# A fused attention and two feed-forward kernel: a fixed cyclic order for each engine in the attention, with its own places for the first weight tiles

## The chip, the cores and the metric

The kernel runs on one core of a Trainium2 chip. Its metric is the device time of one execution in microseconds, as the median of several runs. Five engines take part, and each works through its own instructions in the order in which they stand in the program: TensorE (PE, with its weight loads PEld), VectorE (DVE), ScalarE (ACT), GpSimd (POOL), and SyncE (SP), which here only issues DMAs.

## What is computed

Attention with a threshold, then two feed-forward blocks, all in float32:

```
scores = q @ k^T / 8                          # 4 batches x 8 heads, 576 positions, head size 64
thresh = max(scores, row) - tau
attn   = softmax(where(scores >= thresh, scores, -1e9))
x      = (attn @ v) as 2304 tokens x 512
h      = x @ w_in                             # 512 -> 2048
x      = (h * tanh(softplus(h))) @ w_out      # 2048 -> 512
out    = (silu(x @ w_gate) * (x @ w_val)) @ w_out2     # 512 -> 1536 -> 512
```

## The kernel before

**Precision.** A float32 product is made of three matmuls in the narrower type fp32r: an operand is split into a rounded part ("hi") and the rest ("lo"). A weight tile arrives as 64-bit words and is converted to such a pair by ten operations (`Weights.ops`): a load (l), six operations on DVE (a L437, b L440, c L447, d L450, e L454, x L458), one integer addition on POOL between b and d (u, L444), the hi part on ACT (L463) and the lo part, which is on POOL for the first four tiles and on DVE for the others (L468).

**Attention.** The 32 heads are worked in 16 pairs. A pair p has nine score blocks S0 to S8 of 128 queries by 576 keys (`scores`, tile s, L89 on PE, three buffers). For each block i, DVE takes the row maximum (R, L108), POOL makes the threshold (H, L112), ACT the exponential (E, L118), DVE the masked product with its row sum (M, L126, tile pp). PE transposes pp in 14 groups (T, `trans`, tile tg, L149) and ACT copies each group from PSUM (V, `evac`, L155 to L162) into pt. Two products with v follow (A, `av`, L172), one for each half of the queries, with the reciprocal of the row sums (Q on DVE, L182), its spread (rw on POOL, L189), its transposition (B on PE, tile rg, L197) and copy (C on ACT, L205); DVE multiplies the two (x, L210). The tiles tg, rg and av share two PSUM banks (`g`), which they take in turn in a sequence that is written down in `turns`: a tile must wait until the one before the last has been read. The inputs of a pair are loaded by SP (one buffer for q and k together, `n`), scaled (POOL), split in hi (ACT, L219) and lo (POOL, L222), and copied by DMA into a stacked form (`stack`, tile stk, L231, four copies for q and eight for k).

**The order.** `attention` puts all these operations into a `Plan`, which writes the program. An operation has an engine, an assumed cost, what it must wait for, the buffers that it takes and frees, and a rank. `Plan.run` walks through an assumed time: at each step it takes, of the operations that are ready, the one that can start first, or, within a window `WAIT` of 0.2, the one of the lowest rank. The rank is 9 times the number of the pair plus an entry of the table `RANK` for its kind. Beside the attention stand the conversions of the first four weight tiles (`beside`, tiles wraw, cg, cn, early), with one number for a whole tile (`EARLY`), and the split of the first 512 tokens (x0, L722 and L723, with `XEARLY`). The feed-forward part (`moes`) has a plan of its own behind that of the attention.

The core of `Plan.run`:

```
t, e = min((max(clock[e], o["t"]), o["rank"], o["n"], e) for e in engines for o in ready[e])[::3]
t, _, _, o = min(((max(clock[e], o["t"]), o["rank"], o["n"], o) for o in ready[e]
                  if max(clock[e], o["t"]) <= t + self.wait), key=lambda x: x[1:3])
```

Of the kernel before, what the change touches and what calls it, by code (L numbers as in the profile page):

```python
# [20 lines left out]
def f(ap):  # L21
    return ap.bitcast(F32)
# [22 lines left out]
def attention(tc, cst, q, k, v, x, beside=None, S=576):  # L45
# [14 lines left out]
    st = [dict() for _ in range(NP)]  # L60
# [194 lines left out]
    plan = Plan(SLOTS, WAIT)  # L255
    for p in range(NP):
        ranks = {x: iter(y) for x, y in RANK.items()}
        small = iter(range(16))

        def op(eng, cost, fn, *a, key, after=(), take=(), free=()):  # L260
            kind = "first" if p == 0 and key[0] in ("q", "k") else key[0] if eng != "DMA" else "D" + key[0] if key[1] == "load" else "st"
            plan.op(eng, cost, lambda p=p: fn(p, *a), (p, *key), [(p, *x) for x in after], take, free, 9 * p + next(ranks[kind]))

        if p == 0:
            for h in range(2):
# [22 lines left out]
        for i in range(9):  # L288
            c, h = divmod(i, 2)
# [9 lines left out]
            if i in (3, 8):  # L299
                u = int(i == 8)  # L300
# [16 lines left out]
    if beside:  # L317
        beside(plan, place)
    with tc.manual_schedule():
        plan.run()  # L320
    ctx.close()


class Plan:
# [10 lines left out]
        ACT=dict(PE=.216, DVE=.245, ACT=.145, Pool=.16, DMA=.16),  # L335
        Pool=dict(PE=.143, DVE=.06, ACT=.08, Pool=.096, DMA=.08),
# [17 lines left out]
                    n[x[0]] += 1  # L354
                o[to].append(x)

    def run(self):
        made = {o["key"]: o for o in self.ops}
        took = {x: o for o in self.ops for x in o["take"]}
        gave = {x: o for o in self.ops for x in o["free"]}  # L360
        for o in self.ops:
            o["t"], o["then"] = 0.0, []
        for o in self.ops:
            before = [(made[x], True) for x in o["after"] if x not in self.given]
            for x, k in o["take"]:
                if (x, k - 1) in took:
                    before.append((took[x, k - 1], False))
                if k >= self.slots[x]:
                    before.append((gave[x, k - self.slots[x]], True))
            o["left"] = len(before)  # L370
            for y, late in before:
                y["then"].append((o, late))
        engines = {o["eng"] for o in self.ops}
        clock = {e: 1.3 if e == "DMA" else 0.0 for e in engines}
        ready = {e: [o for o in self.ops if o["eng"] == e and not o["left"]] for e in engines}
        n, turn = 0, False
        while any(ready.values()):
            t, e = min((max(clock[e], o["t"]), o["rank"], o["n"], e) for e in engines for o in ready[e])[::3]
            t, _, _, o = min(((max(clock[e], o["t"]), o["rank"], o["n"], o) for o in ready[e] if max(clock[e], o["t"]) <= t + self.wait), key=lambda x: x[1:3])
# [304 lines left out]
@with_exitstack  # L684
def kern(ctx, tc, q, k, v, tau, w_in, w_out, w_gate, w_val, w_out2, out):
    cp = ctx.enter_context(tc.tile_pool(name="c", bufs=1))
    pe = ctx.enter_context(tc.tile_pool(name="w0", bufs=1))
    NT, DM = out.shape
    acc = cp.tile([P, DM // P * NT], F32, name="acc")
    tc.nc.scalar.preload_act_table_set("natural_log_exp_and_others")  # L690
    cst = consts(tc, cp, tau)


    chunks = [(c, min(CHUNK, NT - c)) for c in range(0, NT, CHUNK)]

    def units(groups, one):
        return [dict(one=one, j=j, c0=c0, n=n, g0=g, G=G, lastg=(g, G) == groups[-1]) for g, G in groups for c0, n in chunks for j in range(g, g + G)]

    starts = lambda sizes: [(sum(sizes[:i]), n) for i, n in enumerate(sizes)]
    gr1, gr2 = starts(GROUPS1), starts(GROUPS2)  # L700
    U1, U2 = units(gr1, True), units(gr2, False)

    tiles = []
    for g, G in gr1:
        for i in range(0, G, 2):
            tiles += [(m, j, m is w_out) for m in (w_in, w_out) for j in range(g + i, min(g + i + 2, g + G))]
    for j in range(w_out2.shape[0] // P):
# [24 lines left out]
CHUNK = 512  # L732
# [57 lines left out]
```

## Time and profile before

| | |
|---|---|
| median of 3 runs | 1168.89 us (1168.82 to 1168.99) |
| the profiled execution | 1168.52 us, of which its span is 1166.7 us |
| PE busy | 1122.5 us, 96% of the span |
| DVE busy | 757.0 us, 65% |
| ACT busy | 457.8 us, 39% |
| POOL busy | 246.1 us, 21% |
| attention | from the start to about 314 us |
| feed-forward | from there to the end, about 852 us |

The span counts from the first to the last instruction; 1.8 us lie around it. The shares are means over stages that differ: in the feed-forward part PE is busy nearly throughout, in the first 40 us hardly. "Busy" of PE counts pipelined matmuls whose ends are modelled. The chain that ended last goes back from the last instruction to what released each step.

### The profile page before, as it was taken

Reading aid. Unit: us, or ns where it says so; the run is one execution under the profiler, and the core shown is the slowest. Engines: PE = TensorE matmul, PEld = TensorE weight load, DVE = VectorE, ACT = ScalarE, POOL = GpSimd, SP = SyncE. Lnnn points to the kernel's source line nnn. Section 1 sums busy time; section 2 is a strip of 40 time slices with the busy share of each in tenths; the row PEclk is TensorE's granted clock in tenths of the full one; section 3 lists DMA queues with packets and bytes.
Section 4 is the critical chain, followed back from the end, with each engine's and each line's share of the span. In section 5 each row is a group of like instructions: output and inputs, shape, how many; then the busy total and the mean of one; then the engine's idle time right before and its main releaser. Section 6 shows DMA issues by size and latency. Waiting matters only on the chain.

```text
span 1166.7 us, 16261 instructions
## 1 busy us (share of the span) xinstructions
PE 1122.5 (96%) x6088; PEld 928.0 (80%) x6088; DVE 757.0 (65%) x1375; ACT 457.8 (39%) x897; POOL 246.1 (21%) x368
## 2 busy tenths in 40 slices
PE   1899999999989999999999999999999999999998
PEld 1677787777667888888888888888888888888887
DVE  7988888888689774582752599636426853594333
ACT  3788777787644332232322245333112211222111
POOL 4555444443373110010110031001000200020000
PEclk9999999999989999999999999999999999999999
DMA  6466566565023211110120111202101210120012
GB/s 190 107 154 163 148 164 158 146 169 146 13 67 104 65 37 37 37 54 19 39 71 1 37 55 58 70 1 72 37 1 37 72 55 1 37 72 1 1 72 91
DMA packets 34271, 83.24 MB, mean 71 GB/s; under 512 B 5264, under 2 KB 5264, under 8 KB 34192
## 3 DMA queue, kind: packets, MB, share of 16 engines
q1 hardware_dynamic: 34192, 82.20, 24.9%
q8 instruction: 48, 0.79, 0.3%
q14 instruction: 31, 0.25, 0.1%
HBM read 50.92 MB, written 4.72 MB: 48 GB/s over the span
## 4 chain that ended last, share of the span: by engine, by line
PE 91%; DVE 5%; POOL 2%; issue 1%; ACT 0%; SPq 0%; DMA 0%; ACTq 0%; DVEq 0%
PE h L525 27%; PE y L536 16%; PE v L525 12%; PE y L538 12%; PE s L89 8%; PE tg L149 7%; PE av L172 7%; DVE cg L454 1%; DVE cn L458 1%; PE rg L197 1%; POOL xlo L552 1%; DVE gl L545 1%; DVE cg L450 1%; POOL cg L444 0%; SPq L76 0%
## 5 line engine op out<-in xcount | busy, mean ns | idle before, releaser
L444 POOL TENSOR_TENSOR cg<-cg,ione 128x512 int32<-128x512 int32 x68 | 92.2, 1360 | 627.9 <-DVE cg L440 627.9
L542 ACT CAST gh<-s 128x512 fp32r<-128x512 f32 (+1 forms) x140 | 80.9, 579 | 257.3 <-DVE s L566 126.4
L525 PE MATMUL h<-xhi,wt 128*128 128x512 f32 (+1 forms) x576 | 170.5, 363 | 0.0
L545 DVE TENSOR_TENSOR gl<-s,gh 128x512 fp32r<-128x512 f32 (+1 forms) x140 | 98.9, 708 | 107.6 <-ACT gh L542 106.3
L89 PE MATMUL s<-stk 128*128 128x320 f32 (+5 forms) x672 | 126.2, 317 | 26.1 <-DVE pp L126 14.2
L566 DVE TENSOR_TENSOR s<-v,u 128x512 f32<-128x512 f32 (+1 forms) x60 | 38.0, 634 | 171.5 <-PE v L525 171.5
L89 PEld LDWEIGHTS s<-stk 128*128 128x128 f32 (+1 forms) x672 | 98.3, 190 | 33.6 <-issue 19.9
L108 DVE TENSOR_REDUCE sm<-s 128x1 f32<-128x576 f32 x144 | 108.6, 754 | 24.6 <-PE s L89 24.4
L525 PEld LDWEIGHTS h<-xhi,wt 128*128 128x128 f32 x576 | 104.7, 189 | 17.3
L126 DVE SCALAR_TENSOR_TENSOR pp<-s,sm,e 128x576 f32<-128x576 f32 x144 | 115.9, 806 | 3.6 <-ACT e L118 1.1
L536 PE MATMUL y<-gh,wt 128*128 128x512 f32 (+1 forms) x400 | 113.3, 368 | 0.0
L118 ACT ACTIVATE e<-s,sm 128x576 f32<-128x576 f32 x144 | 109.3, 759 | 8.8 <-DVE sm L108 8.0
L149 PE MATMUL tg<-idf,pp 128*128 128x128 f32 x656 | 104.6, 285 | 3.5 <-DVE pp L126 2.8
L525 PE MATMUL h<-xlo,wt 128*128 128x512 f32 (+1 forms) x288 | 104.5, 363 | 0.0
L155 ACT COPY pt<-tg 128x384 f32<-128x384 f32 x192 | 87.2, 493 | 33.7 <-PE tg L149 33.4
L525 PE MATMUL h<-xhi,early 128*128 128x512 f32 (+1 forms) x320 | 95.0, 363 | 1.1 <-ACT s L557 1.1
L557 ACT ACTIVATE s<-h 128x512 f32<-128x512 f32 (+1 forms) x80 | 44.2, 555 | 124.6 <-PE h L525 121.8
L149 PEld LDWEIGHTS tg<-idf,pp 128*128 128x128 f32 x656 | 73.2, 142 | 23.2 <-ACT qh L219 4.4
L563 ACT ACTIVATE u<-h 128x512 f32<-128x512 f32 (+1 forms) x60 | 33.2, 554 | 147.9 <-PE h L525 147.9
L172 PE MATMUL av<-pt,vn 128*64 128x256 f32 (+1 forms) x640 | 84.7, 411 | 0.0
L536 PEld LDWEIGHTS y<-gh,wt 128*128 128x128 f32 x400 | 72.6, 189 | 12.5
L575 DVE TENSOR_TENSOR acc<-y,acc 128x512 f32<-128x512 f32 (+1 forms) x100 | 60.6, 633 | 29.7 <-PE y L536 29.7
(110 smaller groups left out, 2162.7 us busy)
## 6 DMA issues: line engine op xcount, KB each, us to landing
raw<-in_dram SPq DMA_DIRECT2D x64, 512.0 KB, 3.5
stk<-kh SPq DMA_DIRECT2D x60, 144.0 KB, 2.7
stk<-kl SPq DMA_DIRECT2D x60, 144.0 KB, 2.6
vn<-in_dram SPq DMA_DIRECT2D x16, 320.0 KB, 2.9
out_dram<-acc SPq DMA_DIRECT2D x18, 256.0 KB, 2.0
qn<-in_dram SPq DMA_DIRECT2D x15, 288.0 KB, 3.2
kn<-in_dram SPq DMA_DIRECT2D x15, 288.0 KB, 3.6
stk<-qh SPq DMA_DIRECT2D x30, 144.0 KB, 3.7
```

Of the source, the lines that this page charges most:

```text
L89: nc.tensor.matmul(out=s[out, c0:c0 + n], lhsT=stk[:, 0, qc:qc + out.stop - out.start], rhs=stk[:, w, kc:kc + n], start=w == 1, stop=w == 2)
L108: nc.vector.tensor_reduce(out=d["nm"][:, i:i + 1], in_=d["s", i], op=ALU.max, axis=AX.X, negate=True)
L118: nc.scalar.activation(out=e, in_=d["s", i], func=AF.Exp, bias=d["nm"][:, i:i + 1])
L126: nc.vector.scalar_tensor_tensor(out=d["pp", c][:, 576 * h:576 * h + 576], in0=d["s", i], scalar=d["th"][:, i:i + 1], in1=d["e", i], op0=A ...
L149: nc.tensor.transpose(g[:, 128 * m:128 * m + 128], d["pp", c][:, o:o + 128], idf)
L155: nc.scalar.copy(out=t[:, m0:m0 + n, 128 * (c % 2):128 * (c % 2) + 128], in_=g[:, 0:n])
L172: nc.tensor.matmul(out=d["av", u][64 * h:64 * h + 64, 0:n], lhsT=d["vn"][:, 5 * h + j], rhs=d["pt", u][:, 5 * h + j if j < 4 else 4, 0:n], ...
L444: nc.gpsimd.tensor_tensor(out=g, in0=g, in1=self.ione.to_broadcast([P, 512]), op=ALU.add)
L525: nc.tensor.matmul(out=un[nm], lhsT=w[:, a, P * d:P * d + P], rhs=parts(x, d, un["c0"], un["n"]), start=d == 0 and k == 0, stop=d == ND - ...
L536: nc.tensor.matmul(out=y[:, 0:un["n"]], lhsT=w[:, a, P * d:P * d + P], rhs=x, start=first and k == 0, stop=last and k == 2)
L538: nc.tensor.matmul(out=y, lhsT=x[:, P * d:P * d + P], rhs=w[:, a], start=first and k == 0, stop=last and k == 2)
L545: V.tensor_tensor(out=un["gl"], in0=un["s"], in1=f(un["gh"]), op=ALU.subtract)
```

## The change

The tables are new, and so is the way in which the attention's plan uses them. `run(True)` no longer looks at which operation could start first: every engine has one queue that is sorted by rank alone, and takes its operations in that order, waiting at the head if need be. The rank is now 17.4 times the pair's number plus the entry of the table, so that every pair has the same order on each engine, shifted by one pair. `EARLY` has a number for each of the ten operations of each of the four early weight tiles, and `XEARLY` one for each of the eight splits of the first tokens. No operation is added or taken away, no tile or buffer count changes, and the plan of the feed-forward part is as it was.

```diff
-            plan.op(..., 9 * p + next(ranks[kind]))
+            plan.op(..., PERIOD * p + next(ranks[kind]))
...
-        plan.run()
+        plan.run(True)
...
+        queue = {e: sorted((o for o in self.ops if o["eng"] == e), key=lambda o: (-o["rank"], -o["n"])) for e in engines}
...
+            if strict:
+                heads = [e for e in engines if queue[e] and not queue[e][-1]["left"]]
+                t, _, e = min((max(clock[e], queue[e][-1]["t"]), queue[e][-1]["n"], e) for e in heads)
+                o = queue[e].pop()
...
-EARLY, XEARLY = (-20, -129.8, 314.6, -292.4,), 202.1
+EARLY = ((-483.86, -338.08, -278.01, -546.43, -122.87, -178.15, -136.83, 70.72, 117.99, 177.97), ...)
+XEARLY = (96.93, 265.74, 98.77, 224.23, 304.99, 281.73, 136.71, 302.44)
...
+PERIOD = 17.4
...
-            W.ops(plan, n, {x: EARLY[n] - 20 * (x == "l") for x in ("l", "a", "b", "u", "c", "d", "e", "x", "h", "")}, ...)
+            W.ops(plan, n, dict(zip(("l", "a", "b", "u", "c", "d", "e", "x", "h", ""), EARLY[n])), ...)
```

The order moves at these places. The changed file has eight lines more ahead of `Weights`, so that L437 to L468 of before are L445 to L476 there.

**DVE, the first score blocks of pair 0.** In s0_1 the first number is the pair, the second the block; cg1 and cn1 are tiles of the early weight tile 1. L108 is R, L126 is M. Before:

```order
L437 TENSOR_SCALAR cg0_111<-wraw0_110 128x512
L437 TENSOR_SCALAR cg1_120<-wraw1_119 128x512
L440 SCALAR_TENSOR_TENSOR cg1_120<-wraw1_119,cg1_120 128x512
L108 TENSOR_REDUCE sm0_157<-s0_0_138 128x1
L108 TENSOR_REDUCE sm0_157<-s0_1_146 128x1
L447 TENSOR_SCALAR cn1_121<-wraw1_119 128x512
L126 SCALAR_TENSOR_TENSOR pp0_0_168,sm0_157<-s0_0_138,sm0_157,e0_0_161 128x576
L450 TENSOR_SCALAR cg1_120<-cg1_120 128x512
L454 SCALAR_TENSOR_TENSOR cg1_120<-wraw1_119,cg1_120 128x512
L458 SCALAR_TENSOR_TENSOR cn1_121<-cn1_121,cg1_120 128x512
L440 SCALAR_TENSOR_TENSOR cg0_111<-wraw0_110,cg0_111 128x512
L447 TENSOR_SCALAR cn0_112<-wraw0_110 128x512
```

Now:

```order
L445 TENSOR_SCALAR cg1_122<-wraw1_121 128x512
L246 TENSOR_TENSOR stk0_108<-kd0_98,stk0_108 64x576
L455 TENSOR_SCALAR cn1_123<-wraw1_121 128x512
L108 TENSOR_REDUCE sm0_156<-s0_0_142 128x1
L108 TENSOR_REDUCE sm0_156<-s0_1_151 128x1
L126 SCALAR_TENSOR_TENSOR pp0_0_175,sm0_156<-s0_0_142,sm0_156,e0_0_167 128x576
L108 TENSOR_REDUCE sm0_156<-s0_2_158 128x1
L126 SCALAR_TENSOR_TENSOR pp0_0_175,sm0_156<-s0_1_151,sm0_156,e0_1_173 128x576
L108 TENSOR_REDUCE sm0_156<-s0_3_182 128x1
L126 SCALAR_TENSOR_TENSOR pp0_1_203,sm0_156<-s0_2_158,sm0_156,e0_2_191 128x576
L108 TENSOR_REDUCE sm0_156<-s0_4_196 128x1
L126 SCALAR_TENSOR_TENSOR pp0_1_203,sm0_156<-s0_3_182,sm0_156,e0_3_210 128x576
```

Before takes 21 of the 24 conversion operations of DVE between the first maximum of pair 0 and the fifth (its last ones stand behind these rows); now none stands there. Of tile 0 the operations a, b, d, e and c, and of tile 1 a and c, stand ahead of the first maximum; x of tile 0 comes behind the seventh M, and 14 of the others among pairs 1 to 13, one or two at a place, with four between the sixth and the ninth R of pair 5. The last two (e and x of tile 3) stand behind R and x of pair 15's last block and first half.

**PE, the second half of a pair's turn**, here the first blocks of pair 9 beside the second product of pair 8. Before:

```order
L89 MATMUL s9_5_2469<-stk9_2113 128x320 x2
L89 MATMUL s9_5_2469<-stk9_2113 128x256 x2
L149 MATMUL tg9_0_0_2487<-idf_63,pp9_0_2400 128x128 x3
L149 MATMUL tg9_0_3_2491<-idf_63,pp9_0_2400 128x128 x3
L89 MATMUL s9_6_2498<-stk9_2113 128x320 x2
L89 MATMUL s9_6_2498<-stk9_2113 128x256 x2
L149 MATMUL tg9_0_6_2506<-idf_63,pp9_0_2400 128x128 x3
L149 MATMUL tg9_1_0_2513<-idf_63,pp9_1_2459 128x128 x3
L89 MATMUL s9_7_2521<-stk9_2113 128x320 x2
L89 MATMUL s9_7_2521<-stk9_2113 128x256 x2
L149 MATMUL tg9_1_3_2528<-idf_63,pp9_1_2459 128x128 x3
L172 MATMUL av8_1_2535<-pt8_1_2337,vn8_2316 64x320 x10
```

Now:

```order
L149 MATMUL tg9_0_0_2451<-idf_63,pp9_0_2381 128x128 x3
L89 MATMUL s9_5_2458<-stk9_2082 128x320 x2
L89 MATMUL s9_5_2458<-stk9_2082 128x256 x2
L149 MATMUL tg9_0_3_2470<-idf_63,pp9_0_2381 128x128 x3
L149 MATMUL tg9_0_6_2476<-idf_63,pp9_0_2381 128x128 x3
L89 MATMUL s9_6_2481<-stk9_2082 128x320 x2
L89 MATMUL s9_6_2481<-stk9_2082 128x256 x2
L149 MATMUL tg9_1_0_2489<-idf_63,pp9_1_2437 128x128 x3
L149 MATMUL tg9_1_3_2494<-idf_63,pp9_1_2437 128x128 x3
L89 MATMUL s9_7_2500<-stk9_2082 128x320 x2
L89 MATMUL s9_7_2500<-stk9_2082 128x256 x2
L172 MATMUL av8_1_2510<-pt8_1_2317,vn8_2295 64x320 x10
```

The first transposition of pair 9 moves ahead of S5, and those that stood as 0_0 with 0_3 and 0_6 with 1_0 now stand as 0_3 with 0_6 and 1_0 with 1_3, so that none is left between S7 and the product av8_1. In the other half of the turn, from av8_1 to S4 of the next pair, PE's order is the same in both.

**ACT, beside it.** e9_2 is the exponential of block 2, pt the copy of a transposition group (V), rs the copy C. Before:

```order
L118 ACTIVATE e9_2_2446<-s9_2_2412,sm9_2359 128x576
L158 COPY pt8_1_2337<-tg8_4_0_2441 128x4x64 x2
L118 ACTIVATE e9_3_2462<-s9_3_2430,sm9_2359 128x576
L205 COPY rs8_1_2474<-rg8_1_2464 128x320
L162 COPY pt8_1_2337<-tg8_4_4_2449 64x64 x2
L118 ACTIVATE e9_4_2484<-s9_4_2452,sm9_2359 128x576
L155 COPY pt9_0_2486<-tg9_0_0_2487 128x3x128
L155 COPY pt9_0_2486<-tg9_0_3_2491 128x3x128
L118 ACTIVATE e9_5_2511<-s9_5_2469,sm9_2359 128x576
L155 COPY pt9_0_2486<-tg9_0_6_2506 128x3x128
L155 COPY pt9_0_2486<-tg9_1_0_2513 128x3x128
```

Now:

```order
L118 ACTIVATE e9_2_2422<-s9_2_2390,sm9_2345 128x576
L158 COPY pt8_1_2317<-tg8_4_0_2417 128x4x64 x2
L162 COPY pt8_1_2317<-tg8_4_4_2426 64x64 x2
L118 ACTIVATE e9_3_2442<-s9_3_2409,sm9_2345 128x576
L205 COPY rs8_1_2456<-rg8_1_2444 128x320
L155 COPY pt9_0_2450<-tg9_0_0_2451 128x3x128
L118 ACTIVATE e9_4_2474<-s9_4_2430,sm9_2345 128x576
L155 COPY pt9_0_2450<-tg9_0_3_2470 128x3x128
L155 COPY pt9_0_2450<-tg9_0_6_2476 128x3x128
L155 COPY pt9_0_2450<-tg9_1_0_2489 128x3x128
L118 ACTIVATE e9_5_2522<-s9_5_2458,sm9_2345 128x576
```

The two copies of tg8_4_4 move ahead of E3 and of C, and the exponential E5 moves behind the copy of tg9_1_0.

On POOL the lo part of k of the next pair moves behind the threshold H2, and on SP the load of the next but one pair's q moves ahead of the eight copies of k into the stack; on SP at the start, the load of the first weight tile moves ahead of q and of half of k.

## Rows read from the trace of the kernel before

**Rows 1.** Page section 4: who holds the chain that ended last, over the span

```profile
PE 91%; DVE 5%; POOL 2%; issue 1%; ACT 0%; SPq 0%; DMA 0%; ACTq 0%; DVEq 0%
```

**Rows 2.** Windows, one pair: us, then busy of PE, PEld, DVE, ACT, POOL

```profile
160.13:177.41 17.28, 17.15 (x132) 13.47 (x134) 14.22 (x33) 13.66 (x30) 7.50 (x17) 1.00 0.61 153
```

**Rows 3.** Windows, DVE alone, at the start of the attention

```profile
5.50:13.90 8.40, 7.41 (x13) 1.00 0.92 323
13.90:46.34 32.44, 30.86 (x51) 1.00 0.41 108
```

**Rows 4.** Lines, DVE, 5.5 to 13.8 us: busy us, mean ns | idle before

```profile
L437 DVE TENSOR_SCALAR cg<-wraw 128x512 int32<-128x512 int32 x2 | 0.7, 411 | 0.0
```

**Rows 5.** Lines, DVE, 13.9 to 46.34 us, the conversions alone

```profile
L458 DVE SCALAR_TENSOR_TENSOR cn<-cn,cg 128x512 f32<-128x512 f32 x4 | 6.8, 1705 | 0.1
L454 DVE SCALAR_TENSOR_TENSOR cg<-wraw,cg 128x512 int32<-128x512 int32 x4 | 3.5, 871 | 0.1
L440 DVE SCALAR_TENSOR_TENSOR cg<-wraw,cg 128x512 int32<-128x512 int32 x3 | 2.1, 687 | 0.1
L437 DVE TENSOR_SCALAR cg<-wraw 128x512 int32<-128x512 int32 x2 | 2.1, 1036 | 0.0
L450 DVE TENSOR_SCALAR cg<-cg 128x512 int32<-128x512 int32 x4 | 1.7, 432 | 0.0
L447 DVE TENSOR_SCALAR cn<-wraw 128x512 int32<-128x512 int32 x4 | 1.7, 416 | 0.0
```

**Rows 6.** Timeline: start us, us; first maxima, pair 1's last stack copy, first av

```profile
13.80 1.55 DVE L108 TENSOR_REDUCE sm<-s 128x1 f32<-128x576 f32 x2
...
28.98 0.59 SPq L231 DMA_DIRECT2D stk<-kh  x1
...
46.34 2.38 PE L172 MATMUL av<-pt,vn 128*64 128x256 f32 x20
```

**Rows 7.** Chain that ended last, within one pair: start us, us, what

```profile
164.66 0.22 PE rg L197 x2
...
165.75 0.66 PE tg L149 x6
...
172.79 0.13 issue
172.92 0.41 PE rg L197 x2
...
174.09 0.80 PE tg L149 x6
...
175.48 0.93 PE tg L149 x6
176.41 0.53 PE s L89 x4
...
177.41 2.84 PE av L172 x19
```

**Rows 8.** Timeline of ACT in the same pair

```profile
173.86 0.42 ACT L162 COPY pt<-tg 64x64 f32<-64x64 f32 x2
...
175.68 0.77 ACT L118 ACTIVATE e<-s,sm 128x576 f32<-128x576 f32 x1
176.31 0.88 ACT L155 COPY pt<-tg 128x384 f32<-128x384 f32 x2
```

**Rows 9.** Timeline, later: a conversion while POOL waits, and POOL (brackets: idle before)

```profile
348.70 0.68 DVE L458 SCALAR_TENSOR_TENSOR cn<-cn,cg 128x512 f32<-128x512 f32 x1
...
351.12 1.42 POOL L444 TENSOR_TENSOR cg<-cg,ione 128x512 int32<-128x512 int32 x1 [2.89 <-DVE cg L440]
```

**Rows 10.** Timeline at the end of the attention: brackets give idle before

```profile
313.96 0.49 DVE L210 TENSOR_TENSOR acc<-av,rs 128x320 f32<-128x320 f32 x1 [5.55 <-PE av L172]
...
315.23 7.66 POOL L552 TENSOR_TENSOR xlo<-acc,xhi 128x512 fp32r<-128x512 f32 x5 [8.21 <-ACT xhi L549]
```

**Rows 11.** DMA issues, 160 to 178 us: KB each, us to landing

```profile
stk<-kh SPq DMA_DIRECT2D x4, 144.0 KB, 2.7
```

More of the change, by code (lines that the diff above doesn't have):

```diff
@@ L261, in op @@
             kind = "first" if p == 0 and key[0] in ("q", "k") else key[0] if eng != "DMA" else "D" + key[0] if key[1] == "load" else "st"
-            plan.op(eng, cost, lambda p=p: fn(p, *a), (p, *key), [(p, *x) for x in after], take, free, 9 * p + next(ranks[kind]))
+            plan.op(eng, cost, lambda p=p: fn(p, *a), (p, *key), [(p, *x) for x in after], take, free, PERIOD * p + next(ranks[kind]))
         if p == 0:
@@ L355, in op, with run @@
                 o[to].append(x)
-    def run(self):
+    def run(self, strict=False):
         made = {o["key"]: o for o in self.ops}
@@ L377, in run @@
         while any(ready.values()):
-            t, e = min((max(clock[e], o["t"]), o["rank"], o["n"], e) for e in engines for o in ready[e])[::3]
-            t, _, _, o = min(((max(clock[e], o["t"]), o["rank"], o["n"], o) for o in ready[e] if max(clock[e], o["t"]) <= t + self.wait), key=lambda x: x[1:3])
+            if strict:
+                heads = [e for e in engines if queue[e] and not queue[e][-1]["left"]]
+                t, _, e = min((max(clock[e], queue[e][-1]["t"]), queue[e][-1]["n"], e) for e in heads)
+                o = queue[e].pop()
+            else:
+                t, e = min((max(clock[e], o["t"]), o["rank"], o["n"], e) for e in engines for o in ready[e])[::3]
+                t, _, _, o = min(((max(clock[e], o["t"]), o["rank"], o["n"], o) for o in ready[e] if max(clock[e], o["t"]) <= t + self.wait), key=lambda x: x[1:3])
             ready[e].remove(o)
@@ L404 @@
 TURN = 0.16
-EARLY, XEARLY = (-20, -129.8, 314.6, -292.4,), 202.1
+EARLY = ((-483.86, -338.08, -278.01, -546.43, -122.87, -178.15, -136.83, 70.72, 117.99, 177.97), (83.95, -59.96, 90.15, 99.11, 59.63, 161.34, 195.41, 211.82, 268.18, 353.64), (90.77, 120.32, 234.39, 218.66, 154.26, 250.85, 252.39, 292.87, 286.81, 297.74), (110.51, 128.14, 159.04, 177.67, 155.41, 208.84, 339.2, 348.67, 441.07, 594.86),)
+XEARLY = (96.93, 265.74, 98.77, 224.23, 304.99, 281.73, 136.71, 302.44)
 SLOTS = dict(wraw=3, wc=6, sm=4, wt=4, s=3, g=2, e=4, pp=3, pt=2, rw=6, rs=6, vn=1, stk=2, n=1, hl=2)
-RANK = dict(P=(-1107.5, -3856.5,), S=(1554.8, 4238.1, -1560.9, 6102.6, 2908.6, 4102, 775.3, 522.3, 4206.5,), R=(-497.8, -3340.3, 669.6, 3608.3, 3026, 717.8, 831.5, 928.3, 4030.3,), H=(-886, -444.4, 1030.3, -4229.5, -2589.8, 349.5, 1807.7, 1355.9, 213.1,), E=(3368.6, 3927.2, 1695.2, -673.1, 1498.6, 1776.5, -593.4, 669.3, -846.5,), M=(-1175.9, 2946.4, 945.8, -609.9, -2796.2, -3324.4, 4863.3, -385.9, -1034.2,), T=(-478.2, 4203, 1183.7, -3198.6, 4629, -1326.8, 1256.1, -915.3, -1499, 4366.2, -87.2, 1989.7, -1057.9, -309.2,), V=(42.7, -4071.5, -346.7, 5127, 3454.4, 6389, -3685.4, 995.6, 2605, 958.3, 1465.4, 344.9, -629.1, 846.5,), Q=(3107.2, -1624.9,), rw=(1354.7, 2037.2,), B=(1328.8, -3213.1,), C=(2643.5, -837.5,), x=(-1547.1, -1257.1,), A=(-860.3, 2598.4, 29.5, 62, 62, 62,), Dq=(520.6,), Dk=(-2288.5,), Dv=(290.4,), q=(932.4, 1295.4, 1207.3,), k=(5062.6, -143.8,), st=(1990.4, -587.4, -280.8, 262.9,), first=(-1663.3, -753.4, -565, -1886.6, -1082, -513.8, -1127.5, -1209, -547.5, -548.2, -763.4, -797.9, 477.9, -1762.2, -1379.4, -1091.3, -1322.9, -672.5,))
@@ new lines @@
+PERIOD = 17.4
+RANK = dict(first=(-150.78, -113.2, -142.86, -586.82, -261.67, -483.31, -79.57, -91.85, -103.43, -30.22, -70.26, -241.87, -475, -167.25, -572.12, -358.96, -89.37, 39.96,), Dv=(104.87,), S=(51.58, 53.03, 55.88, 57.93, 60.26, 61.92, 64.49, 66.32, 67.51,), R=(60.32, 62.49, 63.91, 64.41, 64.83, 66.99, 67.49, 67.88, 74.38,), H=(31.01, 31.63, 33.94, 37.26, 37.57, 42.48, 43.86, 46.73, 47.34,), E=(49.67, 50.13, 52.21, 54.15, 58.31, 61.56, 62.03, 62.51, 66.92,), M=(63.39, 64.14, 64.74, 65.4, 65.77, 69.33, 70.2, 72.29, 79.94,), T=(60.89, 62.99, 63.66, 65.52, 65.67, 67.32, 68.41, 69.58, 69.95, 71.81, 73.46, 74.38, 75.41, 75.54,), V=(57.48, 58.36, 58.69, 60.09, 61.84, 64.65, 65.74, 66.17, 66.77, 68.68, 69, 69.09, 70.12, 71.33,), P=(42.9, 49.1,), Q=(70.19, 81.22,), rw=(43.95, 50.72,), B=(67.86, 78.15,), C=(65.44, 73.17,), A=(73.23, 84.04,), x=(81.26, 87.85,), Dq=(62.1,), q=(6.71, 28.1, 12.36,), Dk=(73.05,), k=(34.04, 17.47,), st=(73.06, 74.1, 80.63, 84.66,))
@@ L718, in beside @@
         for n in range(NEARLY):
-            W.ops(plan, n, {x: EARLY[n] - 20 * (x == "l") for x in ("l", "a", "b", "u", "c", "d", "e", "x", "h", "")}, place, ["wraw"], ["wraw"], ["wc"], ["wc"], "Pool")
+            W.ops(plan, n, dict(zip(("l", "a", "b", "u", "c", "d", "e", "x", "h", ""), EARLY[n])), place, ["wraw"], ["wraw"], ["wc"], ["wc"], "Pool")
         for d in range(DM // P):
             a, h, l = x[:, d, 0:CHUNK], x0[0][:, d], x0[1][:, d]
-            plan.op("ACT", .093 + CHUNK / 1200, lambda a=a, h=h: tc.nc.scalar.copy(out=h, in_=a), ("x0", d), [(d, "x", 0), (d, "x", 1)], [], [], XEARLY)
-            plan.op("Pool", .04 + CHUNK / 418, lambda a=a, h=h, l=l: tc.nc.gpsimd.tensor_tensor(out=l, in0=a, in1=f(h), op=ALU.subtract), ("X0", d), [("x0", d)], [], [], XEARLY)
+            plan.op("ACT", .093 + CHUNK / 1200, lambda a=a, h=h: tc.nc.scalar.copy(out=h, in_=a), ("x0", d), [(d, "x", 0), (d, "x", 1)], [], [], XEARLY[2 * d])
+            plan.op("Pool", .04 + CHUNK / 418, lambda a=a, h=h, l=l: tc.nc.gpsimd.tensor_tensor(out=l, in0=a, in1=f(h), op=ALU.subtract), ("X0", d), [("x0", d)], [], [], XEARLY[2 * d + 1])
     attention(tc, cst, q, k, v, x, beside)
```

## The prediction

> **What bounds the kernel now.** I read the page's chain first: PE holds 91% of it [rows 1], so only a stretch in which PE waits can give anything, and the feed-forward part, which this change leaves as it is, gives nothing. What is left is the attention, some 314 us, and it has two faces. From the first product with v at 46.34 [rows 6] it is a cycle of one turn per pair, 17.28 us each, in which PE is busy 17.15 and DVE 14.22 [rows 2]. Ahead of that, PE hardly works. The windows of DVE show why: between 13.9 and 46.34 us DVE is busy 30.86 of 32.44 us [rows 3], and the lines show that 21 conversions of weight tiles make 6.8 + 3.5 + 2.1 + 2.1 + 1.7 + 1.7 = 17.9 us of it [rows 5]. They stand in DVE's queue among the maxima of the first pair, and every maximum, mask, transposition and product of the attention waits behind them. These weights are wanted only at 314 us.
>
> **Term 1, the start.** DVE's queue is the path from the first maximum at 13.80 to the first av at 46.34 [rows 6]. Of the 21 conversions there, one stays (x of the first tile, one L458). Its two prices are 0.68 us, where POOL waits [rows 9], and 1.7 us, the mean at the start [rows 5]; I take 1.2, between them. So 17.9 - 1.2 = 16.7 us leave the path. Ahead of the first maximum stood two L437 and one L440; now seven operations stand there, four more: d, e and two c, by the means of rows 5 about 0.43 + 0.87 + 0.42 + 0.42 = 2.1 us. DVE was idle 8.40 - 7.41 = 1.0 us in that stretch [rows 3], which they can fill, so 1.1 us are added: 15.6 us of gain, 15.5 for short. The load of the first weight tile now goes ahead of q and half of k and may cost some tenths more. Two bounds. The best is that the kept L458 is short and the four are hidden: 17.9 - 0.7 = 17.2. The worst: pair 1 can't start before its stacks are there. In before the last of these copies is issued at 28.98 and takes 0.59 [rows 6], and such a copy lands 2.7 us after its issue [rows 11]: 32.3; with the score and transposition that stand between, the first av could come at about 33.3, a gain of 13. That chain gets no longer by the change, since it begins with the load and split of pair 1's q and k, on POOL and ACT, from which conversions are taken as well. If the tiles' DVE time is gone, it is this chain that is late next. Ends: -13 and -17.2; taken: **-15.5 us**.
>
> **Term 2, the turn.** In a turn PE loses time at four places that the chain shows: 0.13 of idle time and 0.41 instead of 0.22 for two transpositions of the reciprocals (rg), then 0.80 and 0.93 instead of 0.66 for six transpositions (tg) [rows 7]: 0.73 us. All four lie in the second half, from rg at 172.92 to av at 177.41, 4.49 us. They are waits for one of the two PSUM banks, which ACT empties: each tg waits for the copy of the tile before the last. The rest of the turn keeps its order on PE and shows no such loss. So I follow ACT from 172.92 in the new order, with the steps that the old one shows: E 0.63 (from 175.68 to 176.31), a copy V 0.44 (half of 0.88), the two small ones 0.42 [rows 8]. The order now is small copies, E3, C, V, E4, V, V, V: in before E5 too stood ahead of the copy that av's bank waits for, and now it stands behind. With C as long as a V: 0.42 + 0.63 + 0.44 + 0.44 + 0.63 + 0.44 + 0.44 = 3.44 us to the copy of tg_0_6, so tg_1_3 can start at 176.36; it takes half of 0.66, S7 0.53 [rows 7], and av starts at 177.22 instead of 177.41: 0.19 us. There are 15 such turns: **-3 us**. Ends: none at all, if another of these waits grows by as much; and the whole 0.73, 15 x 0.7 = 10.5 us, if no bank is late.
>
> **Term 3, the conversions in their new places.** 14 of them now lie among pairs 1 to 13: three each of b and d, two each of a, c, e, x. Short (0.69, 0.43, 0.41, 0.42, 0.69, 0.68 [rows 4, 5, 9]) they make 7.8 us, at the means of the start 11.4 us [rows 5]. DVE has 17.28 - 14.22 = 3.06 us idle in a turn [rows 2], and the most that meet are four (b, d and two c, about 2.0 us). The cover is DVE's idle time at the points where it waits for PE; where one stands at a point where PE waits for DVE, it costs its length. Ends: 0 and half of the long sum, 5.7; taken **+0.5**, near the lower end, because the idle time of 13 turns (40 us) is over three times the long sum.
>
> **Term 4, the end of the attention.** The last e and x of tile 3 stand on DVE where it idled 5.55 us for av; the last hi and lo parts fall into the 8.21 us in which POOL waited for ACT [rows 10]. Nothing is added; the feed-forward part then starts as before, from the same state. 0.
>
> Moved on POOL and SP: the lo part of k behind one threshold, a load of 0.3 to 0.6 us ahead of eight stack copies. Both delay the stacks of the next pair, which are wanted only half a turn later; 0.
>
> **The sum:** -15.5 - 3 + 0.5 = -18.0 us. The profiled execution took 1168.52, 0.4 below the median of the runs; 1168.5 - 18.0 = **1150.5 us**. All ends together: 1140.8 and 1161.2.
>
> **The rule that speaks against it.** An L458 takes 1.7 us at the start and 0.68 where POOL waits [rows 5, 9], and POOL is busy 7.50 of each 17.28 us [rows 2]; so the 14 conversions may well meet POOL's work, and be long. The Trainium skill, GPSIMD Engine Reference, section Specifications, says the same as a rule: POOL shares its SBUF interfaces with DVE and contends with DVE instructions that have two SBUF inputs or use both ports. The rows agree with it. By that rule the long sum holds, and rival B is what it makes.
>
> **Rivals.**
> A: the turn does not get shorter, since the waits for the banks only change their place. For it: ACT is busy 13.66 of 17.28 [rows 2], and E3 now stands ahead of C. Only the start gains: 1168.5 - 15.5 + 0.5 = 1153.5.
> B: the conversions in the turns meet POOL and lie on the path whole: 1168.5 - 15.5 - 3 + 11.4 = 1161.4. Against it: the idle time above.
> C, slower: DVE becomes the bound. M4 now stands directly behind M3 and must wait for E4, which on ACT stands behind E3, C and a copy; three maxima follow it in a row, for which PE must be ahead. The price is DVE's idle time at these heads. It takes over where waits pass 3.06 us in a turn, and outweighs the start where they pass it by more than 15.5/15 = 1.0, so at 4.1 us. One E, C and one V make 0.77 + 0.44 + 0.44 = 1.65 [rows 8], under half of that. With 5 us a turn is 19.2 us: 15 x 1.94 = 29 - 15.5, 1182.
> D: the start is held by its loads. The first tile's half megabyte goes ahead of q and k, the first maximum waits for that and the 2.1 us, and the stacks of pair 1 for this: 13 less 2.1, a gain of 11, and no more: 1168.5 - 11 - 3 + 0.5 = 1155.
> That the change does nothing can be left out: the printed order shows the conversions gone from the start.
>
> **How the numbers follow.** The forecast has 0.60, A 0.18, B 0.08, D 0.10, C 0.04. Faster than 0.2% (2.3 us, about what can be told from no change) are all but C: with a little for what none of them names, faster 0.95, same 0.01, slower 0.04. The range goes from 1143, three quarters of the way to the best end, to 1159, which takes in A, D and most of the way to B; C and the rest of B are left out.
>
> **What will show it.** Right: no L458 group of four among the first maxima; the first av at 30 to 32 us; av to av 17.0 to 17.2 us; 852 us from the last av on, as before. Term 1 is wrong if av starts after 34, and then the row to look at is what S1 of pair 1 waits for. Term 2 is wrong if the turn is 17.28 or if the tg groups of six still take 0.8 to 0.9. Term 3 is wrong if turns with conversions are longer than turns without. A turn above 18.3 us would be rival C.

## The result, and the profile after

The changed kernel takes 1150.08 us, the median of five runs (1148.86 to 1151.23), against 1168.89 before (five runs, 1168.80 to 1168.99): a ratio of 0.984 (95% interval 0.9825 to 0.9854). The profiled execution took 1150.61 with a span of 1148.8, so its span is 17.9 us shorter. The forecast was 18.0 less; the total came out almost to the tenth. Its terms did not, as the rows show. Of the runs below, one execution of no_conv, the traced one, took 3945.72 us, with TensorE's matmuls more than twice as long throughout, and is left out.

The chain that ended last, by engine (for [rows 1]):

```profile
PE 90%; DVE 5%; POOL 2%; issue 1%; ACT 1%; DMA 1%; SPq 0%; DVEq 0%; POOLq 0%; ACTq 0%
```

PE holds as much of it as before. What changed lies where PE waited. The timeline of DVE at the start, for [rows 3, 6] (start, us, instruction, idle time before it):

```profile
11.44 1.82 DVE L246 TENSOR_TENSOR stk<-kd,stk 64x576 fp32r<-64x576 f32 x1
...
15.33 1.95 DVE L246 TENSOR_TENSOR stk<-kd,stk 64x576 fp32r<-64x576 f32 x1
...
17.54 0.74 DVE L108 TENSOR_REDUCE sm<-s 128x1 f32<-128x576 f32 x1
...
29.69 0.69 DVE L466 SCALAR_TENSOR_TENSOR cn<-cn,cg 128x512 f32<-128x512 f32 x1
```

The first maximum now comes at 17.54 instead of 13.80, but from there to the first av (33.04) it is 15.5 us instead of 32.54. The one L466 that stayed is short. DVE no longer holds this stretch; another chain now does. In order of time, up to the first av:

```profile
21.02 1.37 POOL kl L222
...
22.42 4.54 DMA qn<-in_dram
...
27.13 0.74 POOL qn L216
27.87 0.25 POOL sm L112
...
29.03 1.48 PE s L89 x10
...
33.11 1.44 PE av L172 x11
```

The lo part of pair 1's k (kl) frees the one buffer in which q and k are split; only then is the load of pair 2's q issued (4.54 us). On POOL its scaling (qn) stands ahead of a threshold (sm) of pair 0, DVE's mask waits for that threshold, and PE for the mask.

One turn in the windows view (as [rows 2]), and its second half in the chain (as [rows 7]):

```profile
59.68:76.52 16.84, 16.72 (x132) 13.39 (x134) 14.29 (x32) 14.62 (x32) 7.32 (x18) 1.00 0.58 159
```

```profile
156.87 0.41 PE rg L197 x2
...
157.45 0.34 PE tg L149 x3
157.79 0.53 PE s L89 x4
158.32 0.82 PE tg L149 x6
159.13 0.53 PE s L89 x4
159.66 0.86 PE tg L149 x6
160.53 0.53 PE s L89 x4
161.06 2.03 PE av L172 x13
```

The turn is 16.84 us. Between rg and av there are 4.19 us instead of 4.49: the groups of six tg still take 0.82 and 0.86, but the group of three that took 0.48 ahead of av now stands behind rg and takes 0.34, and the two s that took 0.59 and 0.58 take 0.53. Another 0.14 is saved in the first half (12.65 instead of 12.79 from av to rg), and that is one group: the three tg ahead of the pair's first product, before and now:

```profile
166.93 0.46 PE tg L149 x3
```

```profile
151.01 0.33 PE tg L149 x3
```

At the end of the attention DVE idles for av as before ([rows 10]: 5.55 us), and the feed-forward part starts 3.58 us after the last av (3.57 before):

```profile
294.14 0.49 DVE L210 TENSOR_TENSOR acc<-av,rs 128x320 f32<-128x320 f32 x1 [4.95 <-PE av L172]
```

### The profile page after: what moved, and what is told of

Same layout as the page of the kernel before. It is cut to its first block, busy times and chain, and to the rows that moved or that the text cites. A ratio compares the mean times of both kernels' runs of the same rounds, so it can differ in the third digit from the quotient of the medians.

```text
span 1148.8 us, 16265 instructions
## 1 busy us (share of the span) xinstructions
PE 1115.2 (97%) x6088; PEld 925.8 (81%) x6088; DVE 753.7 (66%) x1375; ACT 456.3 (40%) x897; POOL 246.7 (21%) x368
## 4 chain that ended last, share of the span: by engine, by line
PE 90%; DVE 5%; POOL 2%; issue 1%; ACT 1%; DMA 1%; SPq 0%; DVEq 0%; POOLq 0%; ACTq 0%
PE h L533 28%; PE y L544 16%; PE v L533 13%; PE y L546 12%; PE s L89 7%; PE av L172 6%; PE tg L149 6%; PE rg L197 1%; DVE cg L462 1%; POOL xlo L560 1%; DVE gl L553 1%; POOL cg L452 1%; DVE cg L458 0%; DVE cn L466 0%; DMA qn<-in_dram 0%
## 5 line engine op out<-in xcount | busy, mean ns | idle before, releaser
L126 DVE SCALAR_TENSOR_TENSOR pp<-s,sm,e 128x576 f32<-128x576 f32 x144 | 115.6, 810 | 11.6 <-ACT e L118 9.6
L533 PEld LDWEIGHTS h<-xhi,wt 128*128 128x128 f32 x576 | 104.7, 189 | 17.4
L108 DVE TENSOR_REDUCE sm<-s 128x1 f32<-128x576 f32 x144 | 105.7, 754 | 16.2 <-PE s L89 16.0
L118 ACT ACTIVATE e<-s,sm 128x576 f32<-128x576 f32 x144 | 103.2, 753 | 7.8 <-DVE sm L108 7.2
L149 PE MATMUL tg<-idf,pp 128*128 128x128 f32 x656 | 102.0, 280 | 0.3
L571 ACT ACTIVATE u<-h 128x512 f32<-128x512 f32 (+1 forms) x60 | 33.3, 555 | 148.5 <-PE h L533 148.5
L544 PEld LDWEIGHTS y<-gh,wt 128*128 128x128 f32 x400 | 72.5, 189 | 12.6
```

The costliest lines, as they stand in the source:

```text
L108: nc.vector.tensor_reduce(out=d["nm"][:, i:i + 1], in_=d["s", i], op=ALU.max, axis=AX.X, negate=True)
L118: nc.scalar.activation(out=e, in_=d["s", i], func=AF.Exp, bias=d["nm"][:, i:i + 1])
L126: nc.vector.scalar_tensor_tensor(out=d["pp", c][:, 576 * h:576 * h + 576], in0=d["s", i], scalar=d["th"][:, i:i + 1], in1=d["e", i], op0=A ...
L149: nc.tensor.transpose(g[:, 128 * m:128 * m + 128], d["pp", c][:, o:o + 128], idf)
L533: nc.tensor.matmul(out=un[nm], lhsT=w[:, a, P * d:P * d + P], rhs=parts(x, d, un["c0"], un["n"]), start=d == 0 and k == 0, stop=d == ND - ...
L544: nc.tensor.matmul(out=y[:, 0:un["n"]], lhsT=w[:, a, P * d:P * d + P], rhs=x, start=first and k == 0, stop=last and k == 2)
```

## The experiments

The table gives the start of the first av, the 14 turns between the starts of the second product (av, u = 1) of pair 0 and that of pair 14, and the median of the runs.

| run | first av | turns | us | ratio to before |
|---|---|---|---|---|
| before | 46.34 | 17.27 to 17.29 | 1168.9 | |
| changed | 33.04 | 16.84, one 17.18 | 1150.1 | 0.984 |
| turn_back | 34.97 | 18.9 to 21.4 | 1187.9 | 1.016 |
| turn_pe | 35.30 | 17.5 to 17.9 | 1161.0 | 0.993 |
| turn_act | 35.70 | 19.4 to 22.2 | 1208.9 | 1.034 |
| turn_dve | 35.16 | 18.1 to 19.6 | 1171.6 | 1.002 |
| turn_old | 36.28 | 17.30 to 18.28 | 1163.8 | 0.995 |
| old_early | 47.64 | 17.29 to 17.81 | 1173.4 | 1.003 |
| conv_early | 46.68 | 16.83 to 16.84 | 1163.1 | 0.995 |
| no_conv | | | 1149.9 | 0.984 |
| tile0_late | 32.45 | 16.84, two longer | 1148.5 | 0.982 |
| start_n2 | 29.80 | 16.84 to 17.07 | 1145.5 | 0.980 |
| after_again | 34.03 | 16.84, one 16.93 | 1149.9 | 0.983 |

**Undoing one engine's order.** First the places that term 2 spoke of, on PE (T) and ACT (E, V) together, in turn_back, and on each alone, in turn_pe and turn_act:

```diff
-T=(60.89, 62.99, 63.66, 65.52, 65.67,    E: 58.31, 61.56, 62.03,    V: 70.12, 71.33,)
+T=(62.0, 62.99, 65.0, 65.52, 66.5,        E: 58.31, 58.5, 62.03,     V: 70.12, 73.5,)
```

> The changed kernel with the second half of a turn back in its old order on two engines: on PE S5 ahead of the first tg, S6 ahead of the third, S7 behind tg_1_0; on ACT E5 ahead of E-independent copies and the small copies behind C. Theory 1 (the turn is shorter because of these orders on PE and ACT): av to av goes back from 16.84 to about 17.28 us, the first av stays at 33.0, total 1150.1 + 15 x 0.44 = 1156.7 (1155 to 1158). Rival (the turn is shorter because of something else, the order of DVE or POOL, or the conversions' places): av to av stays at 16.8 to 16.9, total 1150 to 1151.

> Only PE's second half is back in its old order, ACT keeps the new one. Theory 1a (ACT's order makes the turn short, as in the prediction): av to av at most 16.95, total up to 1152. Rival 1b (PE's order does it: S5 between the first two tg gives a bank its time): av to av 17.2 or more, total 1155 to 1158.

> Only ACT's second half is back in its old order, PE keeps the new one. Theory 1a (ACT's order does it): av to av 17.2 or more, total 1155 to 1158. Rival 1b (PE's order does it): av to av at most 16.95, total up to 1152.

All three came out above every expected total: the old pieces on PE cost 0.73 us a turn in the mean, those on ACT 3.6, both together 2.5, where the whole old cycle was only 0.44 slower than the new one. Not all of the 3.6 is the order. TensorE's granted clock fell to its lower level again and again in turn_act; the turns in which it stayed at 1.00 take 19.4 us, 2.6 more than in the new cycle, and the others are the longer ones. Two turns of turn_act, next to each other (granted clock third from the end):

```profile
68.95:88.38 19.43, 16.91 (x132) 13.47 (x131) 14.32 (x31) 14.82 (x33) 7.46 (x17) 1.00 0.55 138
88.38:109.93 21.55, 19.03 (x133) 14.50 (x132) 14.87 (x33) 14.67 (x32) 8.52 (x18) 0.90 0.50 133
```

In turn_back, too, the turns of 20.0 us and more are those with a lower clock; the others take 18.9 to 19.3. The chain of turn_pe shows how a piece of the old order costs time (one turn):

```profile
147.44 0.34 PE tg L149 x3
...
148.18 0.75 ACT e L118
148.93 0.38 ACT pt L155
...
149.35 0.55 PE tg L149 x3
```

PE wants the bank of the next tg; on ACT an E stands ahead of the copy that empties it. In turn_act the same wait passes through a third engine:

```profile
166.22 0.76 ACT e L118
...
167.07 0.82 DVE pp L126 x2
167.90 0.68 DVE sm L108
...
168.66 0.74 ACT e L118
169.40 0.38 ACT pt L155
```

E4, then on DVE M4 and the maximum behind it, then E5, then the copy that PE's tg waits for: DVE's new order has M4 ahead of R5, and so E5 must not stand early. So the price of one engine's order depends on the others'.

PE's whole order is the old one in turn_pe, but ACT's is not in turn_back and turn_act: E4 still stands behind the copy of tg_0_0 there, as in the new order. ACT's two orders differ at further places than the printed ones, too, and these stay new: E6 behind the copy of tg_1_3, E8 behind those of tg_2_3 and tg_2_6, and E1 ahead of that of tg_3_0. What ACT's whole old order costs alone was not measured.

Then DVE's order alone (turn_dve; its main difference is below, others lie among R1, M8, M0 and M1), and the cycle of before on DVE, ACT, POOL and PE as a set (turn_old):

```diff
-DVE: R4 M3 M4 R5 R6 R7 M5
+DVE: R4 M3 R5 M4 R6 M5 R7
```

> The changed kernel with only DVE's cyclic order taken back (M4 behind R5, M5 behind R6). Theory 1'' (a turn is as short as the worst fit between the orders; DVE's old order then asks for M5 ahead of R7, while ACT gives E5 late): av to av 17.5 us or more, total above 1158. Rival (DVE has 2.5 us to spare in a turn, so its order does not matter): av to av 16.84 to 16.95, total 1150 to 1152.

> The changed kernel, start and conversions as there, but the cyclic order of one pair on DVE, ACT, POOL and PE all taken from the kernel before, word for word (SP keeps the new one). Theory 1' (the four orders belong together, and the old set as a whole costs 17.28 us a turn): first av at 33 to 35, av to av 17.2 to 17.35, total 1156 to 1159. Rival (it was no order but the old planner's choices from pair to pair, or SP's order): av to av at 16.9 or less, total 1150 to 1152.

turn_dve came out on its theory's side: 18.24 us a turn in the mean, although DVE has 2.5 us to spare in a turn. turn_old has the turns that its theory asks for in four cases, 17.30 to 17.33, and no mixture has a turn under 17.5; but ten turns are 17.37 to 18.28, so that the mean (17.61) is no better than turn_pe's 17.57 and the total is 1163.8. The expectation was only half right. Last, the same order with the conversions taken out of the turns:

```diff
-EARLY: b 90.15, 234.39, 159.04   d 161.34, 250.85, 208.84   x 70.72, 211.82, 292.87, 348.67   ...
+EARLY: b 63.82, 63.83, 64.14      d 63.82, 63.83, 64.42      x 63.82, 63.83, 63.83, 64.44      ...
```

> The kernel with the old cycle on DVE, ACT, POOL and PE (as in the run of that name), and in it the 14 conversions back among the first maxima (as in the run with the conversions early). With that run, the changed kernel and the one with the old cycle it makes four cases: old or new cycle, conversions early or late. Theory I (the old cycle without conversions in it is 17.28 us; the conversions made 8 of the 14 turns longer there, since its order leaves no place where they cost nothing): every turn 17.25 to 17.35, the first av at 47 to 49, total 1169 to 1171. Rival (the old cycle is uneven in this kernel by itself, with a first pair in fixed order): turns of up to 17.8 here too, total 1173 or more.

Eight turns are 17.29 to 17.30 now, the others up to 17.81, and 1173.4 is what the rival said. (The edit takes 16 operations back and not 14: e and x of tile 3 as well, which the changed kernel has at the end of the attention.) So the conversions are not the only thing that makes the old cycle uneven. The chain of its third turn names one other:

```profile
97.51 0.21 ACT pt L155
...
97.89 0.62 ACT early L471
...
99.05 0.49 ACT pt L155
...
99.58 0.55 PE tg L149 x3
```

A hi part of a weight tile (L471), which has its place from the new cycle, stands on ACT among the copies that PE waits for. In conv_early the same casts lie in the new cycle, and there every turn is 16.83 to 16.84. This is one turn; what lengthens the others is not shown.

**The start.** In conv_early only the conversions go back, again 16 of them with e and x of tile 3, and the cycle stays new:

> The changed kernel with the 14 conversions on DVE (and the POOL steps between them) back among the first maxima, the loads of tiles 2 and 3 moved up with them; the hi and lo parts stay late. Theory 2 (DVE's queue is the path to the first av): the first av goes from 33.0 to 41 to 45 us, by 7.8 us at the short durations and 11.4 at the long ones, total 1158 to 1162, the turn stays 16.84. Rival (pair 1's loads and stacks hold the first av): the first av at 36 or earlier, total at most 1153.

The first av came at 46.68, 13.6 later, and the total 13.0 higher: the path through DVE is shown, but its price was above my range. The lines of DVE from 17.5 to 46.68 show most of it (count, busy us, mean ns, idle before):

```profile
L466 DVE SCALAR_TENSOR_TENSOR cn<-cn,cg 128x512 f32<-128x512 f32 x4 | 2.8, 690 | 0.1
L455 DVE TENSOR_SCALAR cn<-wraw 128x512 int32<-128x512 int32 x3 | 2.5, 818 | 0.0
L462 DVE SCALAR_TENSOR_TENSOR cg<-wraw,cg 128x512 int32<-128x512 int32 x3 | 2.1, 693 | 0.1
...
L458 DVE TENSOR_SCALAR cg<-cg 128x512 int32<-128x512 int32 x3 | 1.3, 422 | 2.1 <-POOL cg L452 2.1
```

The operations are nearly all short; with L448 (2.1) and L445 (0.8) they make 11.6 us. One L466 (0.7) of these stands there in the changed kernel too, and one L455 (0.4) stood ahead of the first maximum; so the 16 make 10.5, of which e and x of tile 3 are 1.4, and 2.1 more go in waiting for POOL's step between b and d. That is 12.6 of the 13.6; the last 1.0 is open. Set beside turn_old and old_early, taking the conversions out of the start is worth 13.0 us in the new cycle and 9.6 in the old one.

**The conversions in the turns.**

```diff
+            if k in (1, 2, 3) and s and s in "budex":
+                continue
```

> The changed kernel without the steps b, d, e, x and the POOL step of tiles 1 to 3: 12 operations of DVE and 3 of POOL are left out of the turns (the three tiles then hold other numbers). Theory 3 (DVE's idle time hides them, as the prediction's +0.5): total 1149.6 to 1150.1, turns of 16.84 throughout. Rival B (they lie on the path whole): total 1140 to 1145.

1149.9 us (1149.87 to 1150.66) against 1150.1 and 1149.9 of the kernel with them: no difference that can be told. Ten of the 12 operations stand in the turns of the changed kernel, the other two (e and x of tile 3) at the end; the length of the turns without them is not known. Rival B falls.

**What holds the first av now.** The first two lines are tile0_late; start_n2 has the rest too, with the loads of tiles 0 to 2 at 105 to 110 and the conversions of tiles 0 and 1 a turn or so later than in tile0_late (FIX replaces a rank).

```diff
-EARLY = ((-483.86, -338.08, -278.01, -546.43, -122.87, -178.15, -136.83, 70.72, ...
+EARLY = ((80.5, 68.12, 107.55, 116.51, 84.66, 178.74, 212.81, 229.22, ...
...
-SLOTS = dict(... rw=6, rs=6, vn=1, stk=2, n=1, hl=2)
+SLOTS = dict(... rw=6, rs=5, vn=1, stk=2, n=2, hl=2)
+FIX = {(1, 'k', 'load'): 79.6, (1, 'k', 'hi'): 45.6, (1, 'k', 'lo'): 30.5}
```

> The changed kernel with the load of tile 0 behind that of pair 1's q and its conversions, with a and c of tile 1, moved into the turns too (tile 3 follows later, since it takes tile 0's buffer). Theory 4 (what stands ahead of the first maximum is on the path): the first maximum comes at 13 to 14 us instead of 17.5, the first av at 29 to 30 instead of 33.0, total 1146 to 1147. Rival D (pair 1's loads and stacks hold the first av): the first maximum comes as early, the first av not before 32, total 1149 or more.

> The changed kernel with all weight tiles' loads behind pair 1's stacks, no conversion ahead of pair 1's maxima, two buffers instead of one for the q and k being split (one buffer fewer for the copied reciprocals, for room), and pair 1's k load, cast and lo part directly behind those of q. Theory D (with the conversions gone from the start, pair 1's chain of load, split and stack holds the first av): the first maximum at 13.5 to 14, the first av at 29 to 30 instead of 32.5 in the run with tile 0 late, total 1145 to 1147. Rival (the first pair's own waits between ACT, PE and DVE hold it): the first av at 32 or later, total 1148 to 1150.

In tile0_late the first maximum came at 13.72, 3.8 earlier, and the first av only 0.6 earlier. Its chain has the link seen above:

```profile
20.00 4.76 DMA qn<-in_dram
...
24.93 0.75 POOL qn L216
25.68 0.26 POOL sm L112
...
26.84 1.48 PE s L89 x10
...
30.21 1.28 PE tg L149 x6
```

But it lets PE start on this s at 26.84, and in the changed kernel that was at 29.03: 2.2 us earlier. What follows up to the first av is the same work, and it took 5.6 us against 4.0. The six tg took 1.28 where the changed kernel has 0.66, because TensorE's granted clock was at its lower level in this execution (third number from the end):

```profile
28.00:30.00 2.00, 2.00 (x12) 2.00 (x11) 1.14 (x3) 0.85 (x2) 1.25 (x2) 0.58 0.37 139
30.00:32.00 2.00, 2.00 (x11) 2.00 (x11) 0.76 (x1) 0.96 (x3) 0.27 (x1) 0.56 0.85 266
```

So of the 3.8 us, some 1.6 were lost to the clock and 1.6 to the chain, and the first av of 32.45 can't decide between theory 4 and rival D. The link in the chain is another than rival D named: the load of pair 2's q, not pair 1's stacks. In start_n2, with a second buffer, pair 1's k moved up and the tiles' loads and conversions later, that load is off the chain, PE starts on this s at 25.79, and the first av comes at 29.80, as expected. Which of the three moves takes it off was not tested singly. The chain of start_n2 at the same place:

```profile
23.75 0.23 ACT e L118
...
24.39 0.49 ACT pt L155
...
24.91 0.66 DVE pp L126
...
25.79 1.48 PE s L89 x10
```

It is work of pair 0 itself. start_n2 is the fastest of all: 1145.52 us, 0.980 of before (0.9784 to 0.9813), and 4.4 us under after_again, which ran beside it and has its first av 4.2 later.

**The feed-forward part.** It should have been left as it is, but from its first product to the end it took 854.1 us (294.69 to 1148.8) instead of 852.2 (314.50 to 1166.7).

> The changed kernel as it is, profiled once more. Theory C (the 1.6 us lost after the first accumulation in the feed-forward part are TensorE at the 1.2 GHz level for some 4 us at 338 to 342, which does not happen in every execution): from the first feed-forward product to the end 852.3 us if the granted clock stays 1.00 there, 854.1 if it falls; single times spread over 1.5 to 2.5 us. Rival (the new order itself costs it, each time): 854 in this execution too, with the clock at 1.00.

The same kernel took 852.6 there this time. Windows of the changed kernel, then of its second execution (the last three numbers: granted clock, DMA share, GB/s):

```profile
338.00:340.00 2.00, 1.87 (x5) 1.49 (x6) 1.97 (x5) 2.00 (x6) 0.00 (x0) 0.56 0.37 70
340.00:342.00 2.00, 2.00 (x7) 1.57 (x6) 2.00 (x3) 1.08 (x3) 1.42 (x1) 0.58 0.48 193
```

```profile
338.00:340.00 2.00, 1.07 (x5) 0.90 (x6) 2.00 (x5) 2.00 (x5) 0.00 (x0) 1.00 0.26 107
```

In the first, PE waited 2.02 us for ACT to free its accumulator and then ran some 4 us at a granted clock of 0.56 to 0.58, near its lower level of 1.2 GHz: nine matmuls of y took 3.92 us, against 2.34 in before, where the wait was 1.59 and the clock stayed at 1.00. In the second it stayed at 1.00 too, behind a wait of 1.46. The length of the wait is not what decides: in conv_early PE waited 2.02 us at this place as well, and the clock stayed at 1.00:

```profile
351.00:353.00 2.00, 1.67 (x7) 1.41 (x8) 1.97 (x5) 2.00 (x5) 0.00 (x0) 1.00 0.29 43
```

The feed-forward part, whose order is the same in all these runs, took 852.3 to 852.6 us in each of their other traced executions. So the 1.6 us are a matter of the execution, not of the order; the remaining 0.3 to 0.4 were not followed.

## Why the prediction was right, and where it was wrong

By its own terms, in the profiled execution (in brackets the second one, 1148.1):

| term | forecast | measured |
|---|---|---|
| 1, to the first av | -15.5 (-13 to -17.2) | -13.3 [-12.3] |
| 2, the turn | -3 (0 to -10.5) | -6.9 |
| 3, conversions in the turns | +0.5 (0 to 5.7) | +0.4 [+0.25] |
| 4, the end of the attention | 0 | 0.0 |
| feed-forward | 0 | +1.9 [+0.4] |
| sum | -18.0 | -17.9 [-18.6] |

That the total agrees so closely is luck: errors of about 2, 4 and 2 us cancel. That the start and the turn would both gain was right; their sizes were not, nor was the place in the turn. The first av was to come at 30 to 32 us and the turn to be 17.0 to 17.2; they were 33.04 and 16.84.

**Term 1** was mis-sized. Its main part, the DVE time that leaves the path from the first maximum on, was forecast at 16.7, and the stretch became 17.0 shorter, though DVE was no longer what held it. The step that failed is the 1.1 us added ahead of the first maximum: it was 3.7, and 5.0 in the second execution. The last four of DVE's five lo parts of the first q and k (L246) took 5.6 us together, against 4.1 in before; the two of 1.82 and 1.95 ran beside two-input steps of POOL (10.97 to 12.64, 15.25 to 16.67), another, at 13.18, took 0.75. And the load of tile 0 ahead of q stood ahead of those: the second k landed at 10.06 (8.41 in tile0_late, without it), and 1.2 later in the second execution, where the first av too is 1.0 later. tile0_late shows how much of this counts: with the first maximum 3.8 earlier, PE comes to the last stretch before the first av 2.2 earlier; the chain of the next pairs' loads takes back the rest. The worse bound, that pair 1's stacks let no av start before about 33.3, has nearly the measured number (33.04), but by luck: the link that holds is the load of pair 2's q. Rival D, that the loads hold the start and leave it a gain of 11, had the kind of cause right and the link and the size wrong.

**Term 2** was mis-sized by more than half, and by its own sign (groups of six tg that still take 0.8 to 0.9) its mechanism was wrong too. The four places that it names lose nearly what they lost: 0.13, 0.41, 0.82 and 0.86, against 0.13, 0.41, 0.80 and 0.93 (and the 0.13 lies ahead of 172.92, not behind it). The gain came from places that it does not name: from the group of three tg and the two s of the second half, and from the three tg ahead of the first product. "The rest of the turn keeps its order on PE and shows no such loss" failed: 0.14 came from there, 0.30 instead of 0.19 from the second half; with 0.3 in the first pair it is 0.3 + 14 x 0.44 + 0.4 for the last, shorter one = 6.9. That I followed ACT alone was the deeper fault: taking back PE's order, DVE's order or a part of ACT's costs more than the whole old cycle does, so none of them has a price of its own. Which step of the new cycle saves which of these tenths is not shown. Rival A falls (16.84 in every clean turn); rival C as forecast did not come, but its mechanism did in turn_act, where E and M wait for each other and a turn is 19.4 us or more even at full clock: a mixture of the orders, not the change, reaches it.

**Term 3** was right, and conv_early against the changed kernel isolates it: 235.67 and 236.10 us for 14 turns. In the profiled execution 0.34 of it is one turn (17.18), where four conversions meet and one L448 is long:

```profile
114.02 1.71 DVE L448 SCALAR_TENSOR_TENSOR cg<-wraw,cg 128x512 int32<-128x512 int32 x1
```

POOL was taking a lo part (1.41 us from 113.77) then; another L448 in the turns took 0.68. The Trainium skill, GPSIMD Engine Reference, section Specifications, says that POOL shares its SBUF interfaces with DVE and contends with DVE instructions that have two SBUF inputs, as L448 has; the trace agrees, by a factor of 2.5. Yet the long L448 is not what makes the turn long: in the second execution it took 1.72 at the same place, and that turn was 16.93. What differs is an L455 at its start, 0.67 in the first and 0.42 in the second. What the prediction had as cover, DVE's idle time, is only half of it: in the old cycle the same conversions cost 2.2 us (246.52 in turn_old, 244.32 in old_early). There at least one stands where PE is waiting: the chain of turn_old's longest turn (18.28) goes through it.

```profile
172.99 1.65 DVE cn L466
```

**Term 4** held to the hundredth; that the feed-forward part "starts from the same state" did not cover TensorE's clock, which fell at 338 us in one execution and not in the other.

## What to carry to other kernels

Fixed orders on several queues are one design: price them as a set, and not by taking one engine's order back, since a mixture can be far worse than either whole. When a long queue of work is taken off a path, look for the chain that holds next, and in it for single buffers (here the load that waits for the lo part to free its buffer). Before a turn or a start is read as the effect of an order, compare the granted clock of the two stretches. And hold a total that agrees with a forecast against its terms before believing them.

## What was not expected of the hardware

Waits of PE of one to two and a half microseconds were followed by a granted clock at the lower level in some executions and not in others. After 2.02 us in the feed-forward part it was 0.56 to 0.58 for some 4 us, which cost 1.6 us, and after 2.57 us in tile0_late, ahead of the first av, 0.58 and 0.56, which cost as much; in turn_act it fell after many waits of 1.9 us, in turn_back after two of about 1.1. But after waits of 1.99 to 2.27 us in the feed-forward part of turn_old, conv_early, turn_act and old_early it stayed at 1.00. Only after the longest wait, 4.5 us early in the feed-forward part, did it fall in all twelve executions whose clock was traced. No length of a wait that decides it comes out of these rows. How much of the spread of single times (1148.9 to 1151.2) it makes is not shown; the start adds to it, with a first maximum between 17.5 and 19.5 us in the nine traced executions that load tile 0 ahead of q. There a step of DVE on 64 rows (L246) took up to 1.95 us instead of 0.75 beside a two-input step of POOL, and POOL's scaling of q 1.71 instead of 0.74 beside DVE: each engine slowed the other.
